# Scores of batches 3 to 7: one product per head on 64 rows, all heads of a tile together, in a new order of units

## The chip, the cores and the metric

The kernel runs on one core of a Trainium2 chip. The metric is the device time of one execution in microseconds (us). PE is TensorE's matmul, PEld its weight load, DVE VectorE, ACT ScalarE, POOL GpSimd, SP SyncE, whose queue issues nearly all DMAs.

## The reference

Attention over pooled keys and values, then a feed-forward part on all tokens. Eight batches, eight heads, 576 rows (S) of 64; keys and values are averaged over groups of 8, so each query row meets 72 keys.

```python
k_p = k.reshape(B, H, Sp, pool, D).mean(axis=3)
v_p = v.reshape(B, H, Sp, pool, D).mean(axis=3)
scores = scale * np.matmul(q, k_p.transpose(0, 1, 3, 2))
scores = scores - np.max(scores, axis=-1, keepdims=True)
attn = np.exp(scores)
attn = attn / (np.sum(attn, axis=-1, keepdims=True) + 1e-09)
x = np.matmul(attn, v_p)             # then rows x (heads * 64): 4608 x 512
h = x @ w_in                          # 512 x 2048
g = np.maximum(0.01 * h, h)
out = g @ w_out                       # 2048 x 512
```

All in float32.

## The kernel before, in words

**The feed-forward part** is nine chunks of 512 rows. For each of 16 blocks of 128 hidden units, `m1` makes `ph` in one PSUM bank out of 12 matmuls of 512 columns (L944 to L946; operands are split into a high and a low part, three products for each), ACT applies Prelu in place (L949) and casts to `gh` (L952), DVE takes the rest `gl` (L954), and `m2` adds 12 matmuls (L969 to L971) into four banks `acc`. `ph` has two buffers; `m2` runs two blocks behind `m1`. The chunks run as ten "runs", numbered 0 to 9: chunk 0 is cut in two (runs 0 and 2), run 1 is chunk 1, and run n from 3 on is chunk n - 1.

**The attention** of a later chunk is put between those matmuls, unit by unit. PE's order is fixed by hand: each `m1` and `m2` stops twice (a beat, six matmuls), and after beat i of a run the list of units is worked off up to `len(us) * beat // (beats - 4)`, with 64 beats in a run of 16 blocks. The other engines and SP's queue are ordered by a scheduler that simulates the time of the program; it is not bound to the order of the units.

The rows of a batch come in tiles of 128 (the last one of 64, worked as 128) and in two pieces: for batch 3 three tiles and two, for batches 4 to 7 two and three. Beside run 3 lie the rest of batch 2 and the first piece of batch 3; beside run 4 its second piece and the first of batch 4; and so on, to the second piece of batch 7 beside run 8. For batches 3 to 7 (`b >= MOVED`) the units are these, with t the tile, j the piece and g the half of the heads:

- `q{t}` (`turn_q`, L397): DVE turns the tile's queries into `qT`, 128 partitions (two heads of 64 each) x 4 pairs x 128 rows. Behind the last tile of a piece, `load_piece` issues the next piece's 16 query DMAs on SP.
- `sa{t}{g}` (`s_unit`, L481): one PSUM bank `pss`, and for each of two pairs of heads one product on 128 rows (L488): `qT` is the stationary operand, and `kT`, in which the two heads lie block by block with zeros beside them, moves with 144 columns. Then one maximum on DVE (L496) and four exponentials on ACT (L500), each with its sum.
- `sb{t}{g}` (`norm_unit`, L518): two small DVE operations, three products on POOL into `at` (L528, L538), and a DMA of the rows into DRAM (`put_rows`, L553).
- `ld{j}{g}` (`get_blocks`, L562): four DMAs that bring a piece's rows back as blocks of 32 x 32, into the one tile `blocks`.
- `pm{j}{g}` (`p_moved`, L568): DVE turns `blocks` (L570) and ACT and DVE cast and split into `pT` (L574 to L577).
- `au{j}{g}` (`av_unit`, L608): eight matmuls with the values (L619 to L624) into two banks, and casts into the next chunk's `x` (L636, L637).
- `ku`, `vu`, `vp`: keys turned on PE into `kT` (L408 to L420), values split, the remaining eight values spread. `lk` and `lv` load the keys and values of the batch after (L279, L313, L322) and pool them on POOL (L267, L273); they are put into the middle of a run.

`pss`, `pa` (of `au`), `pk` and `pv` share the two banks of the pool `ps_a`, in turn (`bank`, L244).

`line_up_moved` (L806) writes the order. For a piece with three tiles a, z and y it is, each name one unit:

```
sa a0, sb a0, sa z0, sb z0, [pm of the piece before, g=1], sa a1, sb a1, [au of the piece before, g=1],
[vu], q y, sa y0, sb y0, ld 0, sa z1, sb z1, q (next), sa y1, sb y1, q (next), -, [ku], -, pm 0, [vp],
-, -, -, au 0, ld 1
```

and `-` is a unit without work.

Of the kernel before, what the change touches and what calls it, by code (L numbers as in the profile page):

```python
# [10 lines left out]
F32 = mybir.dt.float32  # L11
# [3 lines left out]
AF = mybir.ActivationFunctionType  # L15
ALU = mybir.AluOpType
AX = mybir.AxisListType
# [7 lines left out]
def tile_pooled_attention_ffn(  # L25
# [9 lines left out]
    nc = tc.nc  # L35

    P = 128
    B, H, S, D = q.shape
    POOL = 8
    SP = S // POOL  # L40
# [3 lines left out]
    NK = DM // P  # L44
# [35 lines left out]
    two = ctx.enter_context(tc.tile_pool(name="two", bufs=2))  # L80
# [3 lines left out]
    four = ctx.enter_context(tc.tile_pool(name="four", bufs=4))  # L84
# [12 lines left out]
        out=copies, in_=ident.rearrange("p (h c j) -> p c h j", h=4, c=4), axis=AX.XY, op=ALU.add  # L97
# [6 lines left out]
        out=heads, in_=ident.rearrange("p (h x) -> p h x", h=4), axis=AX.X, op=ALU.add  # L104
# [6 lines left out]
        out=own, in_=ident.rearrange("p (w g x) -> p g w x", w=2, g=2), axis=AX.XY, op=ALU.add  # L111
# [129 lines left out]
    def keys_values(b):  # L241
        return first if b == 0 else (kT, v_whole, None, v_rem) if b == 1 else (kT, later["v"], v_lo, v_rem)

    def bank(b, name):  # L244
        nonlocal turn
        pool, tag = banks[turn % len(banks)] if b == 0 else banks[0]
        turn += 1
        return pool.tile([P, NK, P], F32, tag=tag, name=name)
# [232 lines left out]
    def s_unit(b, t, g, qT):  # L481
# [23 lines left out]
            anchor["act"] = ins  # L505
        return e, sm

    blocks = const.tile([P, 3, 3, P], F32, name="blocks")
    at_turn = 0

# [165 lines left out]
    def attention(b):  # L676

        st = {}
        where = [(j, sum(n for _, n in piece[:i]))
                 for j, piece in enumerate(PIECES[b]) for i in range(len(piece))]  # L680

        def loads():
            start_v, st["v"] = load_v(b)
            st["ks"] = one.tile([P, NK, 2, D], F32, tag="ksum", name=f"ksum{b}")
            st["k", 0] = load_main(b, k, 0, "k")
            st["kr"] = load_k_rem(b)
            q_of[b, 0] = load_q(b, 0)
            st["k", 1] = load_main(b, k, 1, "k")
            for t in range(1, 3):
                q_of[b, t] = load_q(b, t)  # L690
            start_v()
            q_of[b, 3] = load_q(b, 3)

        def keys():
            st["pairs"] = load_pairs(b)

        def values():
            start, st["v"] = load_v(b)
            start()

        def kp(p):
            def f():
                if p == 0:
                    st["pk"] = bank(0, f"pk{b}")
                pool_pair(st["pk"], p, st["pairs"][p])
            return f

        def kd():
            place_pairs(b, st["pk"])

        def lk():
            if b == 2:
                split_tiles()
            st["ks"] = load_k(b)

        def kf(g):
            def f():
                pooled(nc.vector, st["ks"][:, 2 * g : 2 * g + 2], st["k", g], P, 2)
                if g == 0:
                    pooled(nc.vector, kremsum[:64], st["kr"][:, 0:1, :], 64, 2)  # L720
                place_k(b, st["ks"], (2 * g, 2 * g + 1), g == 0)
            return f

        def lv():
            if b == 1:
                with tc.issue_after(anchor["gl"].ins):
                    st["vs"] = st["v"]()
            else:
                st["vs"] = load_v(b)[1]() if b > 1 else st["v"]()

        def ku():
            place_k(b, st["ks"])

        def vu():
            st["parts"] = place_v(b, *st["vs"])

        def vp():
            spread_v(b, st["parts"])

        def qu(t):  # L740
            def f():
                if b > 1:
                    j = where[t][0]
                    st["qT", t] = turn_q(b, j, t)
                    after = pieces_q.index((b, j)) + 1
                    if after < len(pieces_q) and where[t + 1 :][:1] != [(j, where[t][1] + tiles[b][t][1])]:
                        load_piece(*pieces_q[after])
                    return
                st["qT", t] = q_unit(b, t, q_of[b, t])
                after = every.index((b, t)) + 2  # L750
                if after < len(every) and every[after] not in q_of:
                    q_of[every[after]] = load_q(*every[after])
                elif after == len(every) + 1:
                    load_piece(*pieces_q[0])
            return f

        def sa(t, g):
            def f():
                st["e", t, g] = s_unit(b, t, g, st["qT", t])
            return f  # L760

        def sb(t, g):
            def f():
                at = st["at", t, g] = norm_unit(b, t, g, *st["e", t, g])
                if b >= MOVED:
                    j, o = where[t]
                    if o == 0:
                        st["rows", j, g] = scratch(b, j, g)
                    put_rows(b, t, at, st["rows", j, g], o)
            return f  # L770

        def pu(t, g):
            def f():
                j, o = where[t]
                if (j, g) not in st:
                    st[j, g] = piece_tiles(b, j, g)
                p_unit(b, t, g, st["at", t, g], st[j, g], o)
            return f

        def au(j, g):  # L780
            def f():
                av_unit(b, j, g, pT if b >= MOVED else st[j, g])
            return f

        def ld(j, g):
            def f():
                st["ab", j, g] = get_blocks(b, j, g, st["rows", j, g])
            return f

        def pm(j, g):  # L790
            def f():
                p_moved(b, j, g, st["ab", j, g])
            return f

        return {
            "loads": loads, "keys": keys, "values": values, "lk": lk, "lv": lv, "kd": kd,
            **{f"kp{p}": kp(p) for p in range(NK)}, "ku": ku, "vu": vu, "vp": vp,
            **{f"q{t}": qu(t) for t in range(len(where))},
            **{f"{n}{t}{g}": u(t, g) for n, u in (("sa", sa), ("sb", sb), ("pu", pu))
               for t in range(len(where)) for g in range(2)},  # L800
            **{f"{n}{j}{g}": u(j, g) for n, u in (("au", au), ("ld", ld), ("pm", pm))
               for j in range(len(PIECES[b])) for g in range(2)},
            "-": lambda: None, "k0": kf(0), "k1": kf(1),
        }

    def line_up_moved(pieces):  # L806

        out, behind = [], [None, None]
        for m, (b, j) in enumerate(pieces):
            a, z, *y = (tiles[b].index(x) for x in PIECES[b][j])  # L810
            nxt = pieces[m + 1] if m + 1 < len(pieces) else None

            def put(*names):
                out.extend((b, x) for x in names)

            def sa(t, g):
                put(f"sa{t}{g}", f"sb{t}{g}")

            def ahead(i):
                if nxt:  # L820
                    out.append((nxt[0], f"q{tiles[nxt[0]].index(PIECES[nxt[0]][nxt[1]][i])}"))

            if m == 0:
                put("-")
                if j == 0:
                    put("ku", "-")
                put(f"q{a}", f"q{z}")
            sa(a, 0)
            sa(z, 0)
            out.extend(x for x in behind[:1] if x)  # L830
            sa(a, 1)
            out.extend(x for x in behind[1:] if x)
            if j == 0:
                put("vu")
            if y:
                put(f"q{y[0]}")
                sa(y[0], 0)
                put(f"ld{j}0")
                sa(z, 1)
                ahead(0)  # L840
                sa(y[0], 1)
                ahead(1)
            else:
                ahead(0)
                put(f"ld{j}0")
                sa(z, 1)
                ahead(1)
                put("-")
            put("-")
            if nxt and nxt[1] == 0:  # L850
                out.append((nxt[0], "ku"))
            put("-", f"pm{j}0")
            if j == 0:
                put("vp")
            put("-", "-", "-", f"au{j}0", f"ld{j}1")
            behind = [(b, f"pm{j}1"), (b, f"au{j}1")]
        b = pieces[-1][0]
        return out + [(b, "-"), (b, "-"), behind[0], (b, "-"), (b, "-"), (b, "-"), behind[1]]
# [284 lines left out]
```

## Time and profile before

| | |
|---|---|
| time, median of 3 runs (lowest, highest) | 943.4 us (942.42, 946.2) |
| the profiled execution's own time | 941.63 us |
| its span | 939.7 us |
| PE busy | 907.3 us (97%) |
| PEld busy | 755.8 us (80%) |
| ACT, DVE, POOL busy | 411.8, 392.3, 176.1 us |
| moved by DMA | 77.00 MB, mean 82 GB/s |

PE's matmuls are pipelined: the durations that the trace gives for them overlap, so what one costs PE is the distance from its start to the next one's. A busy share is an average over ten runs with different work beside them.

### The profile page before, as it was taken

The page shows a single profiled execution, that of the slowest core. Times are in us where ns is not written, and L with a number is a line of the kernel's source. Part 1 is how long each engine was busy: PE and PEld are TensorE (multiplying, and loading weights), DVE is VectorE, ACT ScalarE, POOL GpSimd, SP SyncE. Part 2 cuts the span into 40 slices and gives each one's busy share as a digit, 9 for nine tenths or more (in the row PEclk, how much of TensorE's full clock was granted, in tenths as well). Part 3 has the DMA queues.
Part 4 walks back from the last instruction along what each step waited for, and adds up shares of the span by engine and source line. Part 5 has one row for each costly group of instructions (what it writes and reads, how often), then busy time and mean ns, then how long its engine had stood idle before and what let it go on. Part 6 is the DMA issues. An engine that isn't in the chain of part 4 may idle for free.

```text
span 939.7 us, 12662 instructions
## 1 busy us (share of the span) xinstructions
PE 907.3 (97%) x4293; PEld 755.8 (80%) x4293; DVE 392.3 (42%) x910; ACT 411.8 (44%) x1304; POOL 176.1 (19%) x329
## 2 busy tenths in 40 slices
PE   4998999999999989999999999999999999999998
PEld 3876788878888868888888888888888888888886
DVE  5799675524343233343244434353335322221111
ACT  4797764535343324343344435443535334223112
POOL 3012110231036520232023112230102001000000
PEclk9899999999999999999999999999999999999999
DMA  9996331242134560753076505840463122101001
GB/s 173 282 241 208 85 93 51 50 112 63 29 91 112 118 112 18 133 83 82 10 124 104 95 22 110 121 73 7 94 86 52 17 62 43 26 1 46 0 1 46
DMA packets 243257, 77.00 MB, mean 82 GB/s; under 512 B 217528, under 2 KB 226744, under 8 KB 243192
## 3 DMA queue, kind: packets, MB, share of 16 engines
q1 hardware_dynamic: 242616, 75.66, 37.6%
q8 instruction: 34, 0.56, 0.2%
q10 hardware_dynamic: 576, 0.52, 0.2%
q14 instruction: 31, 0.25, 0.1%
HBM read 56.56 MB, written 19.60 MB: 81 GB/s over the span
## 4 chain that ended last, share of the span: by engine, by line
PE 78%; DMA 6%; ACT 5%; DVE 3%; SPq 3%; POOL 3%; issue 1%; ACTq 0%; DVEq 0%; POOLq 0%
PE ph L944 12%; PE acc L969 12%; PE ph L946 12%; PE ph L945 12%; PE acc L971 12%; PE acc L970 11%; PE pss L488 3%; SPq L279 2%; DMA vremraw<-in_v_dram 1%; DMA k1raw<-in_k_dram 1%; PE pa L619 1%; ACT e L500 1%; DMA v1raw<-in_v_dram 1%; PE pa L624 1%; ACT w_bits L202 1%
## 5 line engine op out<-in xcount | busy, mean ns | idle before, releaser
L944 PE MATMUL ph<-xh,w 128*128 128x512 f32 x576 | 231.5, 402 | 0.5 <-DVE gl L954 0.5
L969 PE MATMUL acc<-w,gh 128*128 128x512 f32 x576 | 230.3, 400 | 0.0
L946 PE MATMUL ph<-xh,w 128*128 128x512 f32 x576 | 226.0, 392 | 0.6 <-DVE w L215 0.6
L945 PE MATMUL ph<-xl,w 128*128 128x512 f32 x576 | 225.9, 392 | 0.0
L971 PE MATMUL acc<-w,gl 128*128 128x512 f32 x576 | 225.2, 391 | 0.0
L970 PE MATMUL acc<-w,gh 128*128 128x512 f32 x576 | 224.7, 390 | 0.0
L954 DVE TENSOR_TENSOR gl<-ph,gh 128x512 fp32r<-128x512 f32 x144 | 99.0, 688 | 260.6 <-ACT gh L952 260.0
L949 ACT ACTIVATE ph<-ph 128x512 f32<-128x512 f32 x144 | 84.3, 586 | 265.0 <-PE ph L946 265.0
L500 ACT ACTIVATE e<-pss,red 128x72 f32<-128x72 f32 x320 | 98.2, 322 | 94.2 <-DVE red L496 79.8
L946 PEld LDWEIGHTS ph<-xh,w 128*128 128x128 f32 x576 | 108.7, 189 | 24.7 <-DVE w L215 1.0
L971 PEld LDWEIGHTS acc<-w,gl 128*128 128x128 f32 x576 | 108.2, 188 | 23.5
L944 PEld LDWEIGHTS ph<-xh,w 128*128 128x128 f32 x576 | 108.8, 189 | 21.3 <-DVE gl L954 0.9
L945 PEld LDWEIGHTS ph<-xl,w 128*128 128x128 f32 x576 | 108.9, 189 | 20.7 <-DVE xl L637 0.5
L969 PEld LDWEIGHTS acc<-w,gh 128*128 128x128 f32 x576 | 108.3, 188 | 20.8 <-DVE o L1003 0.4
L970 PEld LDWEIGHTS acc<-w,gh 128*128 128x128 f32 x576 | 108.5, 188 | 20.5
L528 POOL TENSOR_TENSOR at<-e,red 128x128 f32<-128x128 f32 x100 | 39.6, 416 | 276.3 <-DVE red L521 103.0
L952 ACT CAST gh<-ph 128x512 fp32r<-128x512 f32 x144 | 84.8, 589 | 3.7
L500 ACT ACTIVATION_READ_ACCUMULATOR e<-pss,red 128x1 f32 x320 | 66.2, 207 | 0.0
L496 DVE TENSOR_REDUCE red<-pss 128x4 f32<-128x288 f32 x80 | 36.2, 453 | 69.2 <-PE pss L488 69.0
L488 PEld LDWEIGHTS pss<-kT,qT 128*128 128x128 f32 x280 | 43.2, 189 | 9.4 <-ACT e L500 2.3
L488 PE MATMUL pss<-kT,qT 128*128 128x144 f32 x280 | 46.0, 286 | 2.6 <-ACT e L500 1.6
L534 POOL TENSOR_TENSOR blocks<-e,red 128x256 f32<-128x256 f32 x24 | 17.6, 732 | 144.6 <-DVE red L521 97.5
(143 smaller groups left out, 805.3 us busy)
## 6 DMA issues: line engine op xcount, KB each, us to landing
w_bits<-in_moe_w_in_dram SPq DMA_DIRECT2D x16, 512.0 KB
w_bits<-in_moe_w_out_dram SPq DMA_DIRECT2D x16, 512.0 KB
out_dram<-o SPq DMA_DIRECT2D x31, 256.0 KB
rows<-at SPq DMA_DIRECT2D x40, 192.0 KB
blocks<-rows SPq DMA_DIRECT2D x40, 120.0 KB
v0raw<-in_v_dram SPq DMA_DIRECT2D x16, 256.0 KB
v1raw<-in_v_dram SPq DMA_DIRECT2D x16, 256.0 KB
blocks<-rows SPq DMA_DIRECT2D x40, 96.0 KB
```

The lines of the kernel that those rows point to most:

```text
L488: nc.tensor.matmul(sc[:, 2 * SP * i : 2 * SP * (i + 1)], qT[:, p, :], kT[:, p, :, :].rearrange("d i s -> d (i s)"), start=True, stop=True,)
L500: ins = nc.scalar.activation(e[:, h, :], scv[:, h, :], AF.Exp, bias=mx[:, h : h + 1], accum_out=sm[:, h : h + 1],)
L528: eng.tensor_tensor(cols[:, :, i, :].rearrange("a (h w) y -> a h w y", h=2), e[:, 2 * i : 2 * i + 2, 0:MAIN].rearrange("a h (w y) -> a h w ...
L944: nc.tensor.matmul(ph, w[:, 0, ks], xh[kk], start=kk == 0, stop=False)
L945: nc.tensor.matmul(ph, w[:, 0, ks], xl[kk], start=False, stop=False)
L946: nc.tensor.matmul(ph, w[:, 1, ks], xh[kk], start=False, stop=kk == NK - 1)
L949: nc.scalar.activation(ph, ph, AF.Prelu, alpha=0.01)
L952: casts.append(nc.scalar.copy(gh, ph))
L954: anchor["gl"] = nc.vector.tensor_tensor(gl, ph, gh.bitcast(F32), op=ALU.subtract)
L969: nc.tensor.matmul(a, gh[:, r], hi, start=first, stop=False)
L970: nc.tensor.matmul(a, gh[:, r], lo, start=False, stop=False)
L971: nc.tensor.matmul(a, gl[:, r], hi, start=False, stop=last)
```

## The change

For batches 3 to 7 a new unit `st{t}` takes the place of `sa{t}0` and `sa{t}1`. It takes two PSUM banks, and for each pair of heads makes one product for the head on partitions 0 to 63 into the first bank and one for the head on partitions 64 to 127 into the second, 64 rows and 72 columns each: eight products in the place of four of 128 rows and 144 columns. DVE takes one maximum for each bank, and ACT makes the eight exponentials, bank by bank; they go into two tiles `e`, so that each `e` has heads of both banks. The zeros in `kT` are no longer read there.

The order of the units is new: `sb{t}0` and `sb{t}1` follow their `st{t}`, empty units stand between the tiles, `ld{j}0` stands behind the last tile's `sb{t}0`, and `q` of the next piece comes later. The lists get longer: 60 units become 64 in runs 5 and 6, 56 become 58 in run 4, 58 become 62 in run 7, 33 become 36 in run 8, 55 become 58 in run 3.

```diff
+    def s_tile(b, t, qT):
+
+        kT = keys_values(b)[0]
+        sides = [bank(b, f"pss{b}_{t}_{i}") for i in range(2)]
+        sides = [x.rearrange("a p x -> a (p x)")[:, : 4 * SP].rearrange("a (p s) -> a p s", s=SP) for x in sides]
+        for p in range(NK):
+            for i, side in enumerate(sides):
+                r = slice(64 * i, 64 * i + 64)
+                nc.tensor.matmul(side[:, p, :], qT[r, p, :], kT[r, p, i, :], start=True, stop=True)
+        e = [two.tile([P, 4, SP], F32, tag="e", name=f"e{b}_{t}_{g}") for g in range(2)]
+        red = [four.tile([P, 2, 4], F32, tag="red", name=f"red{b}_{t}_{g}") for g in range(2)]
+        for i, side in enumerate(sides):
+            mx = red[i][:, 0, :]
+            nc.vector.tensor_reduce(out=mx, in_=side, axis=AX.X, op=ALU.max, negate=True)
+            for p in range(NK):
+                h = 2 * (p % 2) + i
+                nc.scalar.activation(
+                    e[p // 2][:, h, :], side[:, p, :], AF.Exp, bias=mx[:, p : p + 1],
+                    accum_out=red[p // 2][:, 1, h : h + 1],
+                )
+        return [(e[g], red[g][:, 1, :]) for g in range(2)]
...
-            sa(a, 0)
-            sa(z, 0)
+            put(f"st{a}", f"sb{a}0", f"sb{a}1")
             out.extend(x for x in behind[:1] if x)
-            sa(a, 1)
+            put("-", "-")
             out.extend(x for x in behind[1:] if x)
             if j == 0:
                 put("vu")
+            put("-", f"st{z}", f"sb{z}0")
             if y:
-                put(f"q{y[0]}")
-                sa(y[0], 0)
-                put(f"ld{j}0")
-                sa(z, 1)
+                put(f"sb{z}1", f"q{y[0]}", "-")
                 ahead(0)
-                sa(y[0], 1)
-                ahead(1)
+                put("-", f"st{y[0]}", f"sb{y[0]}0", f"ld{j}0", f"sb{y[0]}1")
             else:
+                put(f"ld{j}0", f"sb{z}1")
                 ahead(0)
-                put(f"ld{j}0")
-                sa(z, 1)
-                ahead(1)
-                put("-")
+            put("-")
+            ahead(1)
             put("-")
```

## Rows read from the trace of the kernel before

**Rows 1.** The page: the engines' busy time, share and count, the clock granted to PE in 40 slices of the span, in tenths, and the chain that ended last by engine.

```profile
PE 907.3 (97%) x4293; PEld 755.8 (80%) x4293; DVE 392.3 (42%) x910; ACT 411.8 (44%) x1304; POOL 176.1 (19%) x329
...
PEclk9899999999999999999999999999999999999999
...
PE 78%; DMA 6%; ACT 5%; DVE 3%; SPq 3%; POOL 3%; issue 1%; ACTq 0%; DVEq 0%; POOLq 0%
```

**Rows 2.** The table by stretch, runs 3 to 9 (run 9 has no attention beside it): the stretch, its length, busy time and count of PE, PEld, DVE, ACT and POOL, the granted clock, the share of the DMA engines and GB/s.

```profile
256.60:361.70 105.10, 101.03 (x475) 84.07 (x474) 38.15 (x91) 39.85 (x140) 41.31 (x66) 0.98 0.44 97
361.70:457.70 96.00, 96.00 (x456) 80.41 (x455) 35.48 (x79) 37.87 (x122) 22.38 (x42) 1.00 0.42 77
457.70:555.20 97.50, 97.50 (x464) 81.85 (x463) 40.08 (x95) 41.79 (x142) 23.42 (x46) 1.00 0.46 81
555.20:653.00 97.80, 97.80 (x464) 81.78 (x463) 40.35 (x95) 41.78 (x142) 23.39 (x46) 1.00 0.46 80
653.00:750.50 97.50, 97.50 (x463) 81.84 (x462) 39.33 (x93) 41.53 (x140) 12.02 (x30) 1.00 0.36 60
750.50:843.20 92.70, 92.70 (x426) 77.42 (x425) 24.58 (x50) 31.24 (x92) 6.68 (x18) 1.00 0.18 33
843.20:935.80 92.60, 92.60 (x409) 76.46 (x407) 13.54 (x23) 21.14 (x39) 0.00 (x0) 1.00 0.04 14
```

**Rows 3.** The same table for the instructions on `pss` alone, run 5: length, PE, PEld, DVE, ACT, clock, DMA.

```profile
457.70:555.20 97.50, 6.51 (x40) 6.21 (x40) 4.56 (x10) 13.19 (x80) 1.00 0.46 81
```

**Rows 4.** The timeline in run 6 around one unit of scores: start, duration, engine, line, operation; x4 merges four.

```profile
561.54 0.39 PE L945 MATMUL ph<-xl,w 128*128 128x512 f32 x1
...
561.77 0.39 PE L946 MATMUL ph<-xh,w 128*128 128x512 f32 x1
561.77 0.66 PEld L488 LDWEIGHTS pss<-kT,qT 128*128 128x128 f32 x4
562.00 0.65 PE L488 MATMUL pss<-kT,qT 128*128 128x144 f32 x4
...
562.39 0.49 PE L944 MATMUL ph<-xh,w 128*128 128x512 f32 x1
...
562.71 0.40 PE L945 MATMUL ph<-xl,w 128*128 128x512 f32 x1
```

**Rows 5.** The products that pool batch 1's keys: the timeline's merged loads, and, in the groups by line and form, the loads of this form and of the scores (busy us, mean ns of one).

```profile
32.81 1.87 PEld L301 LDWEIGHTS pk<-ident,k0raw 72*128 72x128 f32 x16
...
L301 PEld LDWEIGHTS pk<-ident,k0raw 72*128 72x128 f32 x16 | 1.9, 192 | 0.0
...
L488 PEld LDWEIGHTS pss<-kT,qT 128*128 128x128 f32 x280 | 43.2, 189 | 9.4 <-ACT e L500 2.3 <-ACT qT L465 1.0 <-DVE kT L420 0.9
```

**Rows 6.** The timeline in run 0: a unit of scores whose first load had waited (in brackets the idle time before and what ended it).

```profile
70.16 0.76 PE L488 MATMUL pss<-kT,qT 128*128 128x144 f32 x4 [0.25 <-ACT e L500]
```

**Rows 7.** The timeline in run 5, from the scores of batch 5's second tile, first half of the heads, to its product with the values; the exponentials are those of the second half.

```profile
509.49 0.65 PE L488 MATMUL pss<-kT,qT 128*128 128x144 f32 x4
...
511.03 2.11 POOL L267 TENSOR_TENSOR v1raw<-v1raw 128x512 f32<-128x512 f32 x2 [3.67 <-DMA v1raw<-in_v_dram]
513.10 0.76 POOL L528 TENSOR_TENSOR at<-e,red 128x128 f32<-128x128 f32 x2
...
514.82 1.70 SPq L553 DMA_DIRECT2D rows<-at  x2
518.99 2.03 SPq L562 DMA_DIRECT2D blocks<-rows  x4
...
524.62 0.31 ACT L500 ACTIVATE e<-pss,red 128x72 f32<-128x72 f32 x1
524.92 0.32 ACT L500 ACTIVATE e<-pss,red 128x72 f32<-128x72 f32 x1
...
530.67 0.97 DVE L570 STREAM_TRANSPOSE blocks<-blocks 128x768 f32<-128x768 f32 x1
533.46 0.48 DVE L577 SCALAR_TENSOR_TENSOR pT_rem<-blocks,marks,pT_rem 128x256 fp32r<-128x256 f32 x1
```

**Rows 8.** The chain that ended last, in order of time, in run 3 ahead of batch 3's first product with the values: start, duration, what.

```profile
319.59 0.71 SPq L391
...
328.25 0.60 SPq L279
...
328.95 4.38 DMA rows<-at
...
334.94 3.58 DMA blocks<-rows
```

**Rows 9.** The timeline of PE there.

```profile
340.53 0.42 PE L619 MATMUL pa<-pT_hi,v_hi 128*128 128x320 f32 x1 [2.84 <-ACT pT_hi L574]
341.73 0.63 PE L622 MATMUL pa<-pT_lo,v_hi 128*128 128x320 f32 x1 [0.78 <-DVE pT_lo L576]
342.16 0.47 PE L623 MATMUL pa<-pT_hi,v_lo 128*128 128x320 f32 x1
...
343.76 0.63 PE L944 MATMUL ph<-xh,w 128*128 128x512 f32 x1
344.19 0.62 PE L945 MATMUL ph<-xl,w 128*128 128x512 f32 x1
344.61 0.43 PE L946 MATMUL ph<-xh,w 128*128 128x512 f32 x1
```

More of the change, by code (lines that the diff above doesn't have):

```diff
@@ L760, in sa, with st_, f @@
             return f
+        def st_(t):
+            def f():
+                st["e", t, 0], st["e", t, 1] = s_tile(b, t, st["qT", t])
+            return f
         def sb(t, g):
@@ L800, in attention @@
                for t in range(len(where)) for g in range(2)},
+            **{f"st{t}": st_(t) for t in range(len(where))},
             **{f"{n}{j}{g}": u(j, g) for n, u in (("au", au), ("ld", ld), ("pm", pm))
@@ L814, in put @@
                 out.extend((b, x) for x in names)
-            def sa(t, g):
-                put(f"sa{t}{g}", f"sb{t}{g}")
             def ahead(i):
```

## The prediction

> **What bounds the kernel now.** I read the page's busy shares, slices and chain first: TensorE (PE) is busy 97% of the span, its granted clock is at nine tenths or more of the higher level (2.4 GHz) in all slices but one, and 78% of the chain that ended last is PE's own work [rows 1]. So a microsecond counts when it is PE's, or when PE waits for it; DVE and ACT at 42 to 44% have room. Next the table by stage. The change touches batches 3 to 7, whose units lie beside runs 3 to 8 (one run is one chunk of 512 rows in the feed-forward part). In runs 4 to 8 PE's busy time equals the stretch: there is no idle time to win, only PE work to save [rows 2]. Run 3 alone of these has 4.1 us in which PE was not busy (105.10 less 101.03). Then the scores: the `pss` instructions are x40 in a run of five tiles, so 8 to a tile (each fp32 product is two weight loads and two matmuls) [rows 3]. What they cost PE is read from starts, since the durations overlap: the last matmul ahead of a unit of four starts at 561.77, the first `pss` at 562.00, and the second matmul behind it at 562.71, where two starts of the large stream lie 0.23 apart [rows 4] (0.226 in run 9, 92.60 us for 409 of them [rows 2]); 0.71 - 0.23 = 0.48 us a unit, 0.12 us for each instruction with 144 columns. A tile has two units, 0.96 us; 25 tiles, **24 us**. That is all that the matmuls of this change can be about.
>
> **What one head's product costs.** Eight products to a tile, two instruction pairs each: 16 matmuls of 72 columns in place of 8 of 144, and 16 weight loads in place of 8. By columns a matmul shrinks to 0.06 us, the load does not shrink: the 128 columns of qT stay. The trace has this very form (72 columns moving, 128 loaded, fp32) in batch 1's keys: 16 loads take 1.87 us, and less the last one's 0.19 that is fifteen starts, 0.112 us each [rows 5], though the streaming of 72 columns is 0.06. The load sets that pace, and it is no shorter on 72 rows than on 128 (192 against 189 ns mean [rows 5]). So the question is whether loads into the upper and the lower half of the array run beside each other. No row of before shows a 64-row instruction, so both bounds stand. All 16 in series: 1.79 us a tile, +0.83, times 25 = **+21 us**. Pairwise side by side: 8 x 0.112 = 0.90 us, -0.06, times 25 = **-1.5 us**. I take the second, because the two halves have their own rows of weights and their own banks, and keep the first as a rival. Below 0.90 it goes only if a load takes less than 0.112 us, which neither form in the trace does.
>
> **Switching between 128 and 64 rows.** New, and not in the trace: twice a tile, 50 times. Lower bound nothing, if the next load still slips in under the running matmul as it does for every `pss` now (the load starts with the matmul before it [rows 4]). Upper bound: the tail of a large matmul, 0.39 - 0.23 = 0.16 us [rows 4], and one load that nothing covers, 0.11: 0.27 us, 14 us in all. The nearest row is a `pss` unit behind a wait: four matmuls span 0.76 us where those behind running work span 0.65 [rows 4, 6], so an uncovered load costs 0.11 us. I take this: 50 x 0.11 = **+5.5 us**.
> The Trainium skill ("TensorEngine Tiling (Array Packing)", Key Properties) speaks against the change here: it states that changing the tiling mode drains the engine. No run yet shows it; by it alone the switch would be nearer the upper bound, and the sum some 8 us higher.
>
> **ACT, DVE, POOL.** The number of exponentials, reductions and products stays. But a tile's eight exponentials now follow each other: they start 0.30 us apart [rows 7], 2.4 us on ACT in place of twice 1.2. Behind them on ACT stand Prelu and the cast of `ph`; PE asks for that `ph` buffer again only after three further groups of 12 matmuls, 8.2 us, so this is covered. The first half of the heads (`e` of g = 0) is complete after six exponentials instead of four, since each bank holds heads of both halves: +0.6 us for the chain below. Both score banks are taken at once, but the next unit that asks for a bank behind a burst comes six beats later at the earliest (a beat is six large matmuls, 1.36 us, so 8.2 us), and the burst's reductions and exponentials end some 4 us behind it. I cost both at nothing; the cover is those beats of large matmuls, and without it each burst would hold PE for what is left of 4 us.
>
> **The order.** A piece's rows go norm, DMA to DRAM, DMA back, DVE transpose, casts, and then `au` on PE, in PE's fixed order. I wrote out the units of each run in both orders and laid them on the beats by the kernel's rule. From the scores of the last tile of a batch's first piece to `au00` there were 18 beats in runs 5 and 6; now 11 (12 in runs 3, 4 and 7). Second pieces keep 12 or more, with `ku` between. Eleven beats are 15.0 us and the burst's 1.0: 16.0 us. What the chain needs is read in run 5: scores at 509.49, second `rows` issue ending at 516.52, four `blocks` issues from 518.99 to 521.02 [rows 7], so the last began at about 520.5; with 3.58 us to its landing, as in run 3 [rows 8], 524.1, then 3.27 us from the transpose to the last of `pT` (530.67 to 533.94 [rows 7]): 527.3, that is 17.8 us, 18.4 with the later exponentials. So 2.4 us are missing. Pooling on POOL was part of it: 2.11 us of it ended as these products began, at 513.10 [rows 7]. Without that the chain needs about 16 us and nothing is missing. Waits between 0 and 2 x 2.4 (runs 5, 6) + 3 x 1.0 (runs 3, 4, 7) = 7.8 us; I take **+4 us**, half, since pooling lies beside some of these chains only.
> SP: the order moves rows' DMAs and `ld` past the 16 query loads of `q` (0.45 to 0.7 us each). In run 3 this queue is what ended last: query and key loads from 319.6 to 328.9, then rows, blocks, transpose, and `au00` at 340.5, PE idle for 2.84 and 0.78 us, and the products and two large matmuls behind it at about half pace [rows 8, 9]. There `q2` now comes two beats later and `au00` at the same beat 52. That wait may grow by 2.7 us or vanish (-4.4 with the slow products); I take 0.
>
> **Sum**: -1.5 + 5.5 + 4 = +8 us. On the profiled execution (941.6 us, a span of 939.7 and 1.9 around it) 949.6; the median of the runs shown is 1.8 us above it: 943.4 + 8 = **951.4 us**.
>
> **Rivals.**
> *Loads in series.* +21 + 5.5 + 3 (the longer bursts give the chain time) = 973 us. For it: the only row of this form has that pace. Against: its loads all went to the same rows.
> *Nothing comes of it.* Loads pairwise, switches free, waits covered: 943.4 - 1.5 to +3, about 943 us. For it: today's kinds of matmul follow each other without a gap.
> *Both halves at full speed* (the other side): a pair of heads in the time of one, 8 x 0.06 = 0.48 us a tile, -12 us, with 4 us of waits 935, without them 931. It needs loads at half the pace of every row here, and wins over 0.5% only while a tile's burst, two switches and share of the waits stay under 0.96 - 4.7/25 = 0.77 us. Against it: [rows 5].
> The Trainium skill ("TensorE: Matmul & The Clock Gate", Part 3) reports 3.07 times the speed for four 32-row products of 512 columns. With so many columns no load shows; the rows here have 72. By that page this rival would be the forecast.
>
> **Chances.** Forecast 0.44, with its own range from the bounds of switch and wait 946 to 963; loads in series 0.22; nothing 0.20; full speed 0.14. The range 935 to 973 leaves out half of the first and half of the last rival, 0.18. A measurement of this kernel tells about 0.5% (4.7 us) from no change. Faster: 0.14. Within: 0.20 and the part of the forecast under 948.1, 0.09, 0.29. Slower: 0.57.
>
> **What would show it.** In the profile after: the starts of the 16 `pss` matmuls of a tile over about 0.9 us (in series 1.8, full speed 0.5); the first large matmul behind a burst, and the first `pss`, late by about 0.1 us each; idle time of `pa` behind `pT_hi` or `pT_lo` in runs 4 to 7, about 1 us a run, none today [rows 2]; run 3 as long as before. The prediction is wrong if loads to different rows are faster than 0.112 us each, if a switch costs several tenths, or if the scheduler orders SP's or POOL's work otherwise than I assume.

## The result and the profile after

| | before | after |
|---|---|---|
| time, median of 9 runs (lowest, highest) | 941.6 us (939.87, 946.2) | 949.05 us (945.69, 954.64) |
| ratio | 1 | 1.0079, 95% interval 1.0061 to 1.0097 |
| the profiled execution, its span | 941.63, 939.7 us | 945.69, 943.8 us |
| PE, PEld busy | 907.3, 755.8 us | 911.2, 751.9 us |
| PE, PEld instructions | 4293 | 4493 |

The kernel became 0.8% slower, some 7.4 us. The profiled execution of after is the shortest of its nine, so its trace shows only 4.1 us of this; where its other executions lose the rest, no trace shows. A first look at the page of after:

```profile
PE 911.2 (97%) x4493; PEld 751.9 (80%) x4493; DVE 397.6 (42%) x910; ACT 410.3 (43%) x1304; POOL 173.7 (18%) x329
...
PE 82%; DMA 5%; DVE 3%; ACT 3%; SPq 3%; POOL 2%; issue 1%; DVEq 0%; ACTq 0%; POOLq 0%
```

Beside [rows 1] little has moved but PE: 200 instruction pairs more (25 tiles x 8) and a larger share of the chain. (DVE is 5.3 us busier with the same number of instructions; at 42% it has room.) The next two fences say where. The first is the table by stretch of after, for run 3 and for runs 4 to 8 together, with the columns of [rows 2]:

```profile
255.90:361.40 105.50, 100.98 (x500) 82.47 (x499) 40.24 (x91) 40.16 (x140) 40.91 (x66) 1.00 0.45 97
...
361.40:847.30 485.90, 485.90 (x2441) 401.15 (x2440) 182.34 (x412) 192.45 (x638) 86.42 (x182) 1.00 0.37 66
```

Runs 4 to 8 took 96.0 + 97.5 + 97.8 + 97.5 + 92.7 = 481.5 us before [rows 2]; they are 4.4 us longer, and PE is busy all of it in both kernels: it has more work there, and waits for nothing. Run 3 is as long as it was, 0.4 us aside. The second fence is the timeline of after around one burst (the 16 matmuls of a tile's scores), to be laid beside [rows 4]; its last line is the tenth large matmul behind the one at 564.80:

```profile
563.10 0.39 PE L966 MATMUL ph<-xh,w 128*128 128x512 f32 x1
563.42 0.97 PEld L516 LDWEIGHTS pss<-kT,qT 64*128 64x128 f32 x16 [0.35 <-issue]
563.42 1.11 PE L516 MATMUL pss<-kT,qT 64*128 64x72 f32 x16
564.47 0.19 PEld L964 LDWEIGHTS ph<-xh,w 128*128 128x128 f32 x1
564.47 0.50 PE L964 MATMUL ph<-xh,w 128*128 128x512 f32 x1
...
564.80 0.39 PE L965 MATMUL ph<-xl,w 128*128 128x512 f32 x1
...
567.10 0.39 PE L991 MATMUL acc<-w,gl 128*128 128x512 f32 x1
```

Read from the last large matmul before to the second one behind, less two large ones: 1.70 - 0.45 = **1.25 us** a tile, and so for all 22 bursts of runs 4 to 8. The prediction gave two units 0.96; with the same starts as here a unit of before is 562.71 - 561.77 - 0.45 = 0.49, two are 0.98 to 0.99. Sixteen loads span 0.97 us; less the last one's 0.19, that is seven steps of 0.112: they go in pairs, one into each half. The rest lies at the two ends. Before, the first load of the scores began with the large matmul ahead of it (561.77 and 561.77 [rows 4]); now it begins 0.32 us after that matmul (563.10, 563.42), where the next large one would have begun after 0.23. And the large load behind the burst begins at 564.47, together with the large matmul that needs it. What is left of the 1.25 us beside 8 x 0.112 = 0.90 is 0.35 us for the two changes of rows, 0.18 each on the average (what the way in and the way out cost by themselves is not shown).

The waits that were feared are not there. Batch 5's second tile in run 5, beside [rows 7]: its scores, the end of a pooling on POOL, the norms' first products on POOL, the rows' DMAs, the blocks' DMAs, the turn, the last of `pT`, and the product with the values:

```profile
521.98 1.11 PE L516 MATMUL pss<-kT,qT 64*128 64x72 f32 x16
...
526.53 0.32 POOL L273 TENSOR_TENSOR vremsum<-vremraw 128x64 f32<-128x64 f32 x1
...
526.81 0.76 POOL L550 TENSOR_TENSOR at<-e,red 128x128 f32<-128x128 f32 x2
...
527.95 1.44 SPq L575 DMA_DIRECT2D rows<-at  x2
530.77 2.05 SPq L584 DMA_DIRECT2D blocks<-rows  x4
...
535.12 0.98 DVE L592 STREAM_TRANSPOSE blocks<-blocks 128x768 f32<-128x768 f32 x1 [3.03 <-DMA blocks<-rows]
...
537.40 0.48 DVE L599 SCALAR_TENSOR_TENSOR pT_rem<-blocks,marks,pT_rem 128x256 fp32r<-128x256 f32 x1
...
539.66 0.28 PE L641 MATMUL pa<-pT_hi,v_hi 128*128 128x256 f32 x1
```

The chain takes 15.9 us to the last of `pT` (521.98 to 537.88), and PE comes 1.8 us later. DVE did wait for the blocks, 3.03 us, but nothing that PE needed stood behind it for too long. Run 6 is closer: there the last of `pT` is ready at 638.04, 16.15 us behind the scores and 0.2 us ahead of the product.

```profile
621.89 1.12 PE L516 MATMUL pss<-kT,qT 64*128 64x72 f32 x16
...
637.56 0.48 DVE L599 SCALAR_TENSOR_TENSOR pT_rem<-blocks,marks,pT_rem 128x256 fp32r<-128x256 f32 x1
...
638.22 0.28 PE L641 MATMUL pa<-pT_hi,v_hi 128*128 128x256 f32 x1
```

### The profile page after: what moved, and what is told of

It is laid out like the page before. It is cut to its first block, busy times and chain, and to the rows that moved or that the text cites. A ratio compares the mean times of both kernels' runs of the same rounds, so it can differ in the third digit from the quotient of the medians.

```text
span 943.8 us, 13036 instructions
## 1 busy us (share of the span) xinstructions
PE 911.2 (97%) x4493; PEld 751.9 (80%) x4493; DVE 397.6 (42%) x910; ACT 410.3 (43%) x1304; POOL 173.7 (18%) x329
## 4 chain that ended last, share of the span: by engine, by line
PE 82%; DMA 5%; DVE 3%; ACT 3%; SPq 3%; POOL 2%; issue 1%; DVEq 0%; ACTq 0%; POOLq 0%
PE ph L964 13%; PE acc L989 13%; PE acc L991 12%; PE acc L990 12%; PE ph L965 12%; PE ph L966 12%; PE pss L516 2%; DMA vremraw<-in_v_dram 2%; SPq L279 1%; PE pa L641 1%; DMA w_bits<-in_moe_w_in_dram 1%; ACT e L500 1%; PE pa L646 1%; PE pa L644 1%; SPq L391 1%
## 5 line engine op out<-in xcount | busy, mean ns | idle before, releaser
L524 ACT ACTIVATION_READ_ACCUMULATOR e<-pss,red 128x1 f32 x200 | 43.1, 216 | 0.0
L659 DVE TENSOR_TENSOR xl<-pa,xh 128x256 fp32r<-128x256 f32 (+4 forms) x68 | 27.5, 407 | 33.1 <-ACT xh L658 31.9
L658 ACT CAST xh<-pa 128x256 fp32r<-128x256 f32 (+4 forms) x68 | 24.4, 363 | 35.7 <-PE pa L646 34.6
```

Source lines behind the costliest of these rows:

```text
L524: nc.scalar.activation(e[p // 2][:, h, :], side[:, p, :], AF.Exp, bias=mx[:, p : p + 1], accum_out=red[p // 2][:, 1, h : h + 1],)
```

## The experiments

Ratios are to the kernel before, run on the same chip (median 941.5 to 942.0). "Burst" is PE's price for one tile's scores, read as above.

| run | what | time, us | ratio, 95% interval |
|---|---|---|---|
| after | 64-row bursts, new order | 949.05 | 1.0079 (1.0061 to 1.0097) |
| e1 | new order alone | 941.57 | 1.0001 (0.9992 to 1.0010) |
| e2 | each burst cut in two | 969.74 | 1.0307 (1.0289 to 1.0325) |
| e3 | lower half first, then the upper | 960.55 | 1.0196 (1.0183 to 1.0209) |
| e4 | all rows, no change of rows | 962.84 | 1.0221 (1.0208 to 1.0234) |
| e5 | e1, later loads in run 3 | 942.0 | 1.0017 (0.9998 to 1.0036) |
| e6 | after, later loads in run 3 | 956.59 | 1.0153 (1.0136 to 1.0171) |
| e7 | before, later loads in run 3 | 939.36 | 0.9973 (0.9965 to 0.9982) |
| e8 | e7, new order in runs 4 to 8 | 937.76 | 0.9958 (0.9944 to 0.9971) |
| e9 | e8 with 64-row bursts in runs 4 to 8 | 943.05 | 1.0022 (1.0008 to 1.0036) |

**e1: the order alone.**

```diff
-                st["e", t, 0], st["e", t, 1] = s_tile(b, t, st["qT", t])
+                for g in range(2):
+                    st["e", t, g] = s_unit(b, t, g, st["qT", t])
```

> The new order of units with the products of before: both units of a tile (four 128-row matmuls of 144 columns each) follow each other in the place of the 64-row burst. Theory A (the burst alone costs: 1.25 us in place of 2 x 0.50, 25 times, +6.2 us; the order is free): within 2 us of the kernel before, and about 6 us under the changed kernel. Rival B (the order costs, through later rows and waits of PE for pT): 2 to 7 us over the kernel before, with idle time of pa behind pT in more runs than run 3.

Theory A holds: no change that the measurement can tell. So the 7.4 us belong to the 64-row products, not to the order taken as a whole. The timeline shows what the burst stands against, eight matmuls of the old form in a row: 509.29 - 507.86 - 0.45 = 0.98 us. (The last line is again the tenth large matmul behind the one at 509.29.)

```profile
507.86 0.39 PE L967 MATMUL ph<-xh,w 128*128 128x512 f32 x1
508.08 1.14 PE L488 MATMUL pss<-kT,qT 128*128 128x144 f32 x8
508.97 0.49 PE L965 MATMUL ph<-xh,w 128*128 128x512 f32 x1
509.29 0.40 PE L966 MATMUL ph<-xl,w 128*128 128x512 f32 x1
...
511.57 0.39 PE L992 MATMUL acc<-w,gl 128*128 128x512 f32 x1
```

And the table by stretch shows that the order does two things that cancel (run 3, then runs 4 to 8): runs 4 to 8 are 1.6 us shorter than before, run 3 is 1.6 us longer.

```profile
256.10:362.80 106.70, 101.26 (x475) 83.70 (x474) 38.36 (x91) 40.16 (x140) 41.20 (x66) 0.98 0.46 95
362.80:842.70 479.90, 479.74 (x2265) 403.14 (x2264) 183.18 (x412) 192.52 (x638) 86.24 (x182) 1.00 0.37 67
```

Against this kernel after's runs 4 to 8 are 6.0 us longer, 0.27 for each of 22 tiles: 1.25 less 0.98.

**e2: two bursts in the place of one.** Pairs 0 and 1 go with `st{t}`, pairs 2 and 3 one beat later.

```diff
-        for p in range(NK):
-            for i, side in enumerate(sides):
+        products((0, 1))
+        return lambda: s_tile_end(sides, lambda: products((2, 3)), b, t)
...
                 def f():
+                if b >= MOVED and g == 0:
+                    st["e", t, 0], st["e", t, 1] = st["end", t]()
```

> The changed kernel with each burst cut in two (pairs 0 and 1, then pairs 2 and 3 one beat later): same products, four changes between 128 and 64 rows a tile in the place of two. Theory A (0.18 us for each change of the rows): two bursts of about 0.81 us in the place of one of 1.25, +0.36 us a tile, 25 times: +9 us over the changed kernel, 956 to 960 us if before is 942. Rival C (the extra 0.36 us of a burst is the start of loads behind a wait, or a price for each instruction, not the change of rows): +0 to +3 us.

The time rose by 20.7 us over the changed kernel, more than twice what either theory gave; yet the price of a burst is theory A's. Each half burst costs 476.83 - 475.57 - 0.45 = 0.81 us, two 1.62, 0.37 more than one of 1.25:

```profile
475.57 0.39 PE L1001 MATMUL acc<-w,gl 128*128 128x512 f32 x1
475.89 0.67 PE L517 MATMUL pss<-kT,qT 64*128 64x72 f32 x8
476.49 0.50 PE L974 MATMUL ph<-xh,w 128*128 128x512 f32 x1
476.83 0.39 PE L975 MATMUL ph<-xl,w 128*128 128x512 f32 x1
```

That is 9 us. The other 11 or so are waits: run 3 is 112.30 us (its wait for `pT_hi` is 4.9 us, where after has 2.07), and in runs 4 to 8, where after has none, PE waits for copies out of `acc` (first row: who waited for whom, total, times, longest) and for `pT`.

```profile
255.80:368.10 112.30, 104.52 (x499) 84.70 (x498) 38.71 (x91) 40.11 (x140) 41.05 (x66) 0.97 0.43 91
```

```profile
PE acc L999 <- DVE o L1033: 4.2, 3, 2.0
PE pa L652 <- DVE pT_lo L606: 1.2, 2, 0.8
PE pa L649 <- ACT pT_hi L604: 0.4, 1, 0.4
```

So with the scores complete one beat later there are waits for `pT`, the ones that the prediction feared; the order of after is just early enough, as run 6 showed. The wait for the copies was in no theory; what held the copies up was not followed.

**e3: one half after the other.**

```diff
-        for p in range(NK):
-            for i, side in enumerate(sides):
+        for i, side in enumerate(sides):
+            for p in range(NK):
```

> The changed kernel with the four heads on rows 0 to 63 first, then the four on rows 64 to 127. Theory A (loads run beside each other only when neighbours in PE's order go to different halves): 16 x 0.112 = 1.79 us and the two changes' 0.36: 2.15 us a burst, +0.9 a tile, 25 times: +22 us over the changed kernel. Rival D (the queue looks far enough ahead to pair them whatever their order): the burst stays at 1.25 us and the time at that of the changed kernel.

Neither theory: the burst costs 470.80 - 468.60 - 0.45 = 1.75 us, between theory A's 2.15 and D's 1.25. The 16 loads span 1.47 us:

```profile
468.60 0.39 PE L991 MATMUL acc<-w,gl 128*128 128x512 f32 x1
468.92 1.47 PEld L516 LDWEIGHTS pss<-kT,qT 64*128 64x128 f32 x16 [0.35 <-issue]
468.92 1.62 PE L516 MATMUL pss<-kT,qT 64*128 64x72 f32 x16
470.47 0.50 PE L964 MATMUL ph<-xh,w 128*128 128x512 f32 x1
470.80 0.39 PE L965 MATMUL ph<-xl,w 128*128 128x512 f32 x1
```

Side by side they took 0.97, in series (e4) they take 1.98. So some of the upper half's loads ran beside the lower half's, and not all: 1.47 less the last load's 0.19 is 11.5 steps of 0.112, between the 7 of pairs and the 15 of a series. How far ahead of its matmul a load may start is not shown by this one run. Alternating the halves is worth 0.5 us a tile. The time, 11.5 us over after, fits 25 x 0.50 = 12.5.

**e4: the same products on all rows.**

```diff
-                nc.tensor.matmul(side[:, p, :], qT[r, p, :], kT[r, p, i, :], start=True, stop=True)
+                nc.tensor.matmul(side[:, p, :], qT[:, p, :], kT[:, p, i, :], start=True, stop=True)
```

> The changed kernel with each head's product on all 128 rows (the other head's rows of kT are zeros there), so 16 loads and 16 matmuls of 72 columns without a change of rows. Theory A (loads in series at 0.112 us; no change of rows, so no 0.36): 1.79 us and the 0.1 us that any unit of scores costs the matmul behind it, about 1.9 us a tile, 0.65 more than the burst, 25 times: +16 us over the changed kernel; the first load starts with the matmul before it. Rival C (the start of a burst costs the same whatever its rows): 2.15 us, +22 us.

Theory A: 472.79 - 470.55 - 0.45 = 1.79 us, which is 16 x 0.112 and nothing beside; the first load begins at 470.55, with the large matmul ahead of it. The time, 13.8 us over after, is 25 x (1.79 - 1.25) = 13.5. So the 0.35 us that a burst of after has beyond its loads are there only where the rows change.

```profile
470.55 0.39 PE L990 MATMUL acc<-w,gl 128*128 128x512 f32 x1
470.77 1.90 PE L515 MATMUL pss<-kT,qT 128*128 128x72 f32 x16
472.48 0.48 PE L963 MATMUL ph<-xh,w 128*128 128x512 f32 x1
472.79 0.39 PE L964 MATMUL ph<-xl,w 128*128 128x512 f32 x1
```

```profile
470.55 1.98 PEld L515 LDWEIGHTS pss<-kT,qT 128*128 128x128 f32 x16
```

**e5, e6, e7: run 3's waits.** One line, in the new order with the old products, in after, and in before:

```diff
-            mid = len(us) // 2
+            mid = len(us) - 10 if n == 3 else len(us) // 2
```

> The new order with the products of before (128 rows), and in run 3 the units lk and lv of batch 4 (its key and value loads and their pooling) ten units from the end of the list instead of in its middle. Theory A (run 3's waits of PE come from those loads standing on SP, POOL and DVE's queue ahead of batch 3's queries and rows): run 3 falls from 106 to 97 to 101 us, the time by 3 to 8 us to 934 to 938, with two units of scores in a row saving 0.1 us a tile beside. Rival E (run 3 waits for the length of its own chain): no change, 941 to 942.

> The changed kernel with the same later loads in run 3. Theory A: its bursts still cost 1.25 us against 0.99 for two units in a row, 25 times 0.26 = 6.6 us, so 6 to 7 us over the kernel with the products of before and the same loads, 941 to 945. If the order or the chain of rows had a part in the loss, the distance is another.

> The kernel before with the same later loads in run 3. Theory A: run 3 at 97 to 101 us, the time 935 to 940, about 2 us over the new order with the products of before (0.1 us for each of 25 units of scores less that PE turns to). Rival E: no change.

Mostly a miss. Only before gained (2.7 us: run 3 fell to 102.80). In the new order nothing was won, and after lost another 7 us: its run 3 grew to 114.70, while its runs 4 to 8 stayed where they were (485.70). PE's idle time there has two places (e6; in brackets the idle time before and what ended it):

```profile
332.65 0.79 PE L964 MATMUL ph<-xh,w 128*128 128x512 f32 x1 [3.81 <-DVE gl L974]
350.28 0.64 PE L641 MATMUL pa<-pT_hi,v_hi 128*128 128x320 f32 x1 [4.83 <-ACT pT_hi L596]
```

The edit doesn't move the loads by much: SP still issues the first of batch 4's at 292.79 in e7 and at 293.57 in e6, where before has 292.85, since the scheduler orders that queue by its own simulation. And the loads that stand at 326 to 329 ahead of batch 3's rows in [rows 8] are the sixth of eight sets in the trace, batch 5's, whose units the edit leaves alone. So theory A, that such loads hold up run 3, was not tested. What the edit changes is what stands between them, and run 3's length with that, from 102 to 115 us over these kernels. Which place in the queue decides it was not found. It also means that e5 and e6 don't compare the products alone; e8 and e9 do, with run 3 held nearly equal.

**e8, e9: run 3 held, the two forms of product in runs 4 to 8.** Both have e7's edit and, for run 3, the order of before:

```diff
     def line_up(pieces):
+        if pieces == [(3, 0)]:
+            return line_up_before(pieces)
```

> Run 3 as in the kernel before with the later place of batch 4's loads; runs 4 to 8 in the new order with the products of before, two units in a row. Theory A (the new order saves 0.3 to 0.4 us in each of runs 4 to 8, since PE turns to the scores half as often, and spoils that in run 3): 1.6 to 2 us under the kernel with the old order and the later loads, 937 to 938 us, under both kernels of the case. Rival E (the order is free or costs elsewhere): 939 to 940.

> The same, with the 64-row bursts of the changed kernel in runs 4 to 8 (22 tiles) and run 3 untouched. Theory A (the burst alone costs, 1.25 against 0.99 us): 22 x 0.26 = 5.8 us over the kernel with two units in a row, 943 to 944. If the loss of the changed kernel lay in run 3 to a good part, less than 4 us.

By the times, theory A in both. Runs 4 to 8 of e8, then of e9:

```profile
359.00:839.40 480.40, 479.93 (x2265) 403.35 (x2264) 183.51 (x412) 192.48 (x638) 86.03 (x182) 1.00 0.37 67
```

```profile
359.50:846.40 486.90, 486.23 (x2442) 401.44 (x2441) 182.73 (x412) 192.34 (x638) 86.29 (x182) 1.00 0.36 66
```

6.5 us of stretch, 5.3 us between the medians, where 22 x 0.26 = 5.8 were expected. So the loss stands where run 3 has no part in it. e8, without any 64-row product, is the fastest of all: 0.9958, under before and under after. Its gain over e7, 1.6 us between medians of different chips, is at the edge of what these runs can tell, and the traces place only half of it where theory A has it: runs 4 to 8 are 0.8 us shorter than e7's 481.20, run 3, whose order is e7's, 0.9.

## Why the prediction was right, and where it was not

The forecast was slower by 8 us, and it became slower by 7.4. The total is nearer than its terms, and that is luck: one was too small by 3, another too large by 4. (The lower end of the forecast's range, 946, is not the sum of its lower bounds either: with switch and waits at nothing the sum is 942, which it listed as a rival.)

**The loads bound the product: right, to the number.** The step read 0.112 us a load from the key-pooling rows [rows 5], said that the half matmul doesn't help because 128 columns must be loaded for each head all the same, and took loads pairwise. Seven steps in 0.78 us are 0.112 a pair; in series (e4) it is 0.112 a load. The rival of loads in series is out, as is full speed: a pair of heads costs what it cost before, so the 64-row form had 0.98 - 0.90 = 0.08 us a tile to win, 2 us in all.

**The change of rows: right in kind, too small.** Taken at 0.11 us each, with bounds 0 and 0.27, it measured (1.25 - 0.90)/2 = 0.18 us: e2 with twice as many changes adds 0.37 a tile, e4 without any has none. The nearest row, an uncovered load behind a wait [rows 6], was the wrong neighbour: it has one late load, where a burst starts late (563.42, when the next large matmul would have begun at 563.33) and the large load behind it starts late too, together with its matmul. This is the term that was mis-sized: 50 x 0.18 = 8.8 in place of 5.5 us.
The Trainium skill ("TensorEngine Tiling (Array Packing)", Key Properties) says that a change of tiling mode drains the engine; the trace agrees nearly, with the first load 0.32 us behind the start of the last large matmul in place of none, which is 0.07 us ahead of the end that the profile gives that matmul (563.10 and 0.39). By that rule alone the switch was to be nearer the upper bound of 0.27; at 0.18 it is midway between that and the value taken.

**The waits for `pT`: wrong.** The step gave 0 to 7.8 us and took 4; runs 4 to 8 of after have no idle time of PE, and e1 puts the whole order at 0 +- 0.9 us. It failed in the length of the chain. The beats were nearly as laid out: between `st1` and `au00` there are eleven in run 6 and twelve in run 7, as forecast, and twelve in run 5 and thirteen in runs 3 and 4, one more than forecast. But even run 6's eleven were enough, since the chain needs 16.15 us there and 15.9 in run 5, not 18.4. It was not POOL that had become free: in run 5 the norms again begin as a pooling ends (526.53 and 0.32, 526.81), and from the scores to the rows' DMAs it takes 5.97 us where [rows 7] have 5.33, 0.6 more as the prediction said. Shorter are the way from there to the blocks' DMAs (2.82 us in place of 4.17), from those to the turn (4.35 in place of the 5.1 that were put together with run 3's 3.58), and from the turn to the last of `pT` (2.76 in place of 3.27). Why the two DMA ways are shorter is not shown. That the cover is thin is seen in run 6's 0.2 us, and in e2, in which the chain begins a beat later and PE waits.

**The base was too low**: two units cost 0.98 to 0.99, not 0.96, and the reading stops too soon. The ten large matmuls behind a unit of before follow each other a little slower than others, 2.32 us for ten (562.71 [rows 4] to the line below) where ten undisturbed ones take 2.27; behind two units in a row (e1) it is 2.28, behind a burst 2.30.

```profile
565.03 0.39 PE L971 MATMUL acc<-w,gl 128*128 128x512 f32 x1
```

As a mean over runs 4 to 8 this is 0.05, 0.02 and 0.04 us more, so a tile's scores cost 1.08 us before (two units), 1.00 in a row and 1.29 as a burst. For 22 tiles that makes the order 1.8 us shorter and after 4.5 us longer than before; the stretches say 1.6 and 4.4. So the new order does save PE time by fewer turns to the scores, as e8's expectation has it, and in e1 run 3 takes it back. In the prediction's terms, with these sizes: 25 x (1.25 - 0.98) = 6.8 us for the products and 0 for the order as e1's medians have it, against 7.4 measured (interval 5.7 to 9.1).

**Run 3** was taken at 0, with -4.4 to +2.7. In the profiled executions it has 105.10 before and 105.50 after. e1's 106.70 and e7's 102.80 are within the bounds, but e2's 112.30 and e6's 114.70 show that small changes of the order can move this run by more; in the median of after, which is 3.4 us over the profiled execution, a part may lie there. That is left open.

## What to carry to other kernels

Before a product is cut into halves of the array to run two at a time, look at what sets its pace: where the stationary operand is as wide as before and the moving one is cut to half, two loads side by side take the time of one, and the old form, with zeros beside each block and twice the columns, had already paid for just that. Count the changes of row size too: each costs 0.18 us on the average here beside 512-column matmuls, so they want long bursts, and a burst of 0.9 us is short. And measure a chain in the stage where it will run: the chain to `pT` was put together from one stretch of run 5 and a DMA of run 3, and came out 2.5 us too long.

## What the runs showed of the hardware beyond that

- Loads to different halves of the array run side by side even without alternating strictly: with all of one half ahead of the other (e3) the 16 loads take 1.47 us, between 0.97 and 1.98.
- After an idle stretch in run 3 PE's granted clock was at the lower of its two levels (1.2 and 2.4 GHz) for some of what follows, but not each time: its mean over run 3 is 0.98 before, with 4.0 us of PE's waits in all, 2.84 the longest [rows 2, 9], 0.96 in e6 with 10.1 (4.83 the longest), and 1.00 in after's profiled execution with 4.6 (2.07 the longest).
